# The order of VectorE's routing work in a linear attention with experts behind it, with POOL's tables in the third step and inputs loaded three items deep

## The chip, the cores and the metric

The kernel runs on one core of a Trainium2 chip. TensorE (PE, with its weight loads shown as PEld), VectorE (DVE), ScalarE (ACT), GpSimd (POOL) and SyncE (SP) each execute their own instructions in the order in which the program issues them, and wait for each other on semaphores; DMA transfers are issued from the queues of SP, ACT and POOL. The metric is device microseconds (us) of the whole program, the median of several runs. Before the change it is 382.65 us (3 runs, 382.16 to 382.88).

## The reference

A recurrent linear attention over 4 sequences, 8 heads, 768 tokens and a head dimension of 48, whose output is the input of a top-1 mixture of 8 experts (384 to 1024 to 384). A token keeps the expert of the token before it when its local gate is at least 0.5.

```python
for t in range(S):
    kt, vt, rt = (k[:, :, t], v[:, :, t], r[:, :, t])
    cur = np.einsum('bhd,bhe->bhde', u[None] * kt, vt)
    y[:, :, t] = np.einsum('bhd,bhde->bhe', rt, state + cur)
    state = w[None, :, :, None] * state + np.einsum('bhd,bhe->bhde', kt, vt)
...
for s in range(S):
    fresh_e = int(np.argmax(logits[b, s]))
    if s == 0 or local_gate[b, s] < 0.5:
        e = fresh_e
    else:
        e = prev_e if prev_e >= 0 else fresh_e
    prev_e = e
    ...
    h = np.maximum(x[b, s] @ w1[e], 0.0)
    out[b, s] = p[e] * (h @ w2[e])
```

## The kernel before

The attention works on 16 items, one for each sequence and pair of heads. An item is cut into 6 chunks of 128 tokens. Inside a chunk the scores (keys times queries, L288) are masked by `kept` (VectorE, `am`, L290) and multiplied with the values on PE (`inside`, L297); across chunks, PE sums keys and values of each chunk into T, a part of the PSUM bank `mp` (`added`, L248), a scan on VectorE turns T into the states S (`states`, L254), and PE multiplies them with the decayed queries `rw` (`before`, L310). The bonus term u is `own`: PE sums the product `pd` over the head dimension (L267) and VectorE multiplies it with the values vT (L273). POOL makes `rw`, `ke` and `pd` of the next item (`scale`, L212, L216, L229) and VectorE makes the scaled keys `kw` (`keys`, L236). Each result goes through ACT (L318) and is turned by PE (`turn`, L329), copied by ACT (L331) and stored to x_d. After the four items of a sequence, `logits` (L342, PE) and its copy lT (L343, ACT), then `token_logits` (L348 PE, L349 VectorE) give the gate logits `lt`.

The loop `run` (L352) goes over steps n = 0 to 16. Nothing is scheduled by the framework: the order of the source is the order on every engine. Step n does own(n), the scores of a later item, inside(n-1) and before(n-1), scale(n+1) on POOL and, from step 5, keys(n+2). Score tiles take turns on two pairs of PSUM banks (`banks`); turn, logits and token_logits use the same pairs, so each has to wait until the last reader of its pair is done.

Routing of the first two sequences (group 0; g = 8 in `run`) is woven into steps 9 to 15: `experts_of` (maximum L688, equality L689, its product with `down` L692, then L694 to L696), `keys` and `runs` (a transpose L703 and a scan L708), `turn_runs` (L713, into the last columns of `mp`), `last` (L720), `one_hot` (L727 to L731), `counts` (two matmuls into `mp`, L740 and L741), `ranks` (the ACT copy `ext` L747, the scan `exc` L748, `pos` and `far` L750 to L756), `slots` (L792 to L795), `columns` (`eqv`, L800), `numbers` (POOL, L805), `places` (`ohq`, L811, in two halves) and `summed` (L818). Its constants are made in `constants`, called in steps 3, 4 and 5: small integer tables by POOL's iota (L623), and memsets by VectorE; ACT casts the tables in step 6. The same functions are run again for group 1 in the experts' part, where POOL has no attention work.

Inputs come by SP: `load` (L189) issues rk (queries and keys of an item, 768 KB), kv (584 KB) and vT (384 KB) in this order. rk and vT have AHEAD buffers, kv has AHEAD + 1. Before the loop AHEAD - 1 items are loaded, then the small `wp`; step n loads item n + AHEAD - 1. A load into a buffer waits for that buffer's last reader: POOL's and VectorE's work on rk, the product in own on vT, inside on kv.

Behind step 16 the experts' part gathers tokens by indirect DMA and runs two small units and eight larger ones, bound by PE.

Of the kernel before, what the change touches and what calls it, by code (L numbers as in the profile page):

```python
# [14 lines left out]
Alu = mybir.AluOpType  # L15
# [5 lines left out]
P = 128  # L21
# [5 lines left out]
E, F = 8, 1024  # L27
DK, FK = D // P, F // P
NCH = S // P
NC = B * NCH  # L30
N = B * S

ST = 4
# [4 lines left out]
EARLY = 2  # L38
HEAD = 192
TAIL = 256  # L40
# [8 lines left out]

W_LO, W_HI = 0.8, 1.25  # L50
C2 = NCH // 2
AHEAD = 4
VB = NCH * 2 * DH


def spread(ap, axis, n):

    a = ap.unsqueeze(axis)
    return a.to_broadcast([n if i == axis else s for i, s in enumerate(a.shape)])


class Attention:
# [289 lines left out]
    def run(self, router, fetch, heads):  # L352


        def pair(name):
            t = self.banks(name)
            return [t[:, 0], t[:, 1]]

        M = B * HP

        mp, mp_end = router.mp, 2 * P + 2 + (NCH - 1) * DH

        g = GROUPS[0][1] * HP
        for n in range(M + 1):
            if n + AHEAD - 1 < M:
                self.load(n + AHEAD - 1)
            if n == 0:
                self.scale(0)
                self.keys(0)
                self.tables()  # L370
                self.scores(0, 0)()
                self.scores(0, 1)()
                self.own(0)
                self.nc.scalar.copy(self.first, self.tab[:, 1, 0])
                self.turn_ends(slice(1, HP))
                self.warm(3)
                self.added(0)
                self.reciprocals(1)
                self.states(0)
                self.scale(1)  # L380
                continue
            if n < 3:

                self.keys(n)
                self.inside(n - 1)
                self.before(n - 1)
                if n == 2:
                    self.turn(0, pair("tp"))
                self.nc.scalar.copy(self.first, self.tab[:, n + 1, 0])
                self.scores(n, 0)()  # L390
                keep = self.scores(n, 1)
                self.own(n)
                keep()
                self.added(n)
                self.states(n)
                if n == 1:
                    self.reciprocals(2)
                self.scale(n + 1)
                continue
            if n < M:  # L400
                self.turn(n - 2, pair("tp"))
                if n >= M - 2:
                    fetch(2 * (n - M + 2))
                if n == 3:
                    self.reciprocals(3)
                if n < 5:
                    self.keys(n)
                if n > 3:
                    if n not in (g + 3, g + 5):
                        self.added(n)  # L410
                    self.states(n)
            if n == 4:
                self.keys(5)
            if n > HP and n % HP == 1:
                self.token_logits(n // HP - 1, pair("lq")[0])
            if n == g + 1:
                router.experts_of(0, (0,))
            if n == g + 5:
                router.slots(0)
                router.columns(0)  # L420
            if n == M:
                router.shares(0)
            if n + 1 < M:
                self.scale(n + 1)
            if n == g + 6:
                router.numbers(0, self.nc.gpsimd)
            if 3 <= n < 6:
                router.constants(n - 3)
            if n == M:
                self.turn(M - 2, [self.spare[:, 0], self.spare[:, 1]])  # L430
            self.inside(n - 1)
            if n == g + 3:

                router.turn_runs(0, mp[:, mp_end:])
            self.before(n - 1)
            if M - 2 <= n < M:
                fetch(2 * (n - M + 2) + 1)
            if n == 6:
                router.cast()
            if n == M:  # L440
                break
            if n == g + 3:
                router.last(0, mp[:, mp_end:])
                router.one_hot(0, (0,))
            if n == g + 7:

                router.summed(0, 0)
                router.copied(0, self.nc.vector.tensor_copy)
                self.spare = self.py.tile([P, 2, 512], F32, name="y")
                router.head(self.spare[:, 0])  # L450
                heads()

            ahead = n if n < 5 else n + 1
            if n == 3:
                self.added(3)
                self.states(3)
            if ahead < M:
                self.scores(ahead, 0)()
                keep = self.scores(ahead, 1)
            if n % HP == 0:  # L460

                keep()
                self.own(n)
                self.logits(n // HP - 1, pair("lp")[0])
                if n == 4:
                    self.scores(5, 0)()
                    self.scores(5, 1)()
                    self.keys(6)
                if n == g + 4:
                    self.added(n + 1)  # L470
                    router.counts(0, [mp, mp[:, E * NC // 2:]])
                    router.ranks(0, (0,))
                if n > 4:
                    self.keys(n + 2)
                if n == g + 4:
                    router.ranks(0, (1,))
            else:
                self.own(n)
                if n == g + 2:
                    self.added(n + 1)  # L480
                    router.keys(0, mp)
                    router.runs(0)
                if 4 < n < M - 2:
                    self.keys(n + 2)
                if ahead < M:
                    keep()
            if n == g + 1:
                router.experts_of(0, (1,))
            if n == g + 3:
                router.one_hot(0, (1,))  # L490
            if n == g + 5:
                router.places(0, 0)
            if n == g + 6:
                router.places(0, 1)
        self.inner.close()
# [81 lines left out]
class Router:  # L577
# [43 lines left out]
    def iota(self, name, shape, pattern, base=0, cm=0, cast=False):  # L621
# [5 lines left out]
        self.casts.append((f, i))  # L627
        return f

    def constants(self, part):  # L630
        nc = self.nc
        if part == 0:
            self.ie = self.iota("ie", [P, E], [[1, E]])
            self.iq = self.iota("iq", [P, P], [[1, P]])
            self.ij = self.iota("ij", [P, E * ST], [[1, E * ST]])
            self.ones = self.tl("r_ones", [P, P])
            nc.vector.memset(self.ones, 1.0)
        elif part == 1:
            self.down = self.iota("down", [P, E], [[-1, E]], base=E, cast=True)

            self.t8 = self.iota("t8", [P, NC], [[E * P, NC]], base=2 * E, cm=E, cast=True)
            self.t1 = self.iota("t1", [P, NC], [[P, NC]], base=1, cm=1, cast=True)
        else:

            c = self.g[0]["nc"]
# [5 lines left out]
            nc.vector.memset(self.go, 1.0)  # L651
            nc.vector.memset(self.go.rearrange("p (b c) -> p b c", c=NCH)[:, :, NCH - 1:], 0.0)
            nc.vector.memset(self.g[0]["ext"][:, :, 0:1], 0.0)

            self.tie = self.tl("tie", [P, E])
            for x, (z, base) in enumerate(((slice(0, EARLY), E - 1 - E * TAIL), (slice(EARLY, E), E - 1 - EARLY))):
                i = self.iota(f"tie{x}", [P, z.stop - z.start], [[-1, z.stop - z.start]], base=base)
                self.casts.append((self.tie[:, z], i))
            self.ief = self.iota("ief", [1, E], [[1, E]], cast=True)

            self.size = self.tl("size", [1, E])
            for i, n in enumerate(BLOCKS):
# [18 lines left out]
    def experts_of(self, i, parts=(0, 1)):  # L681

        nc, g, lt = self.nc, self.g[i], self.lt
        lg = lt[:, g["z"], :E]
        if 0 in parts:
            nc.vector.memset(lt[:, g["z"]].rearrange("p (b c) e -> p b c e", c=NCH)[0:1, :, 0, E:], -1.0)
            mx = self.mp[:, :g["nc"]] if i == 0 else g["mx"]
            nc.vector.tensor_reduce(mx, lg, axis=AX.X, op=Alu.max)  # L688
            nc.vector.tensor_tensor(g["eq"], lg, spread(mx, 2, E), op=Alu.is_equal)  # L689
            if i == 0:  # L690
                nc.scalar.copy(g["mx"], mx)
            nc.vector.tensor_tensor(g["eq"], g["eq"], spread(self.down, 1, g["nc"]), op=Alu.mult)  # L692
        if 1 in parts:
            nc.vector.tensor_reduce(g["k"], g["eq"], axis=AX.X, op=Alu.max)  # L694
            nc.vector.tensor_tensor(g["k"], self.t8[:, g["z"]], g["k"], op=Alu.subtract)
            nc.vector.scalar_tensor_tensor(g["key"], lt[:, g["z"], E], FRESH_TO, g["k"],  # L696
                                           Alu.is_le, Alu.mult)
# [1048 lines left out]
```

## Time and profile before

| what | us |
|---|---|
| median of the runs | 382.65 |
| the profiled execution | 383.9 |
| span of the profiled execution | 382.2 |
| PE busy | 367.5 |
| DVE busy | 250.6 |
| POOL busy | 151.3 |
| ACT busy | 107.5 |
| the attention's part of the span, from its start to the experts' first transposes on PE (L1090) | 113.7 |

The span runs from the first to the last instruction of one profiled execution; the rest of its time lies around the span. A profile row "engine line waited for" names who waited and who ended the wait, with the total, the number and the longest. Spans on POOL are rough, and the ends of matmuls are modelled.

### The profile page before, as it was taken

How to read it: one execution, taken by the hardware profiler on the slowest of the kernel's cores; microseconds unless marked ns; L12 is line 12 of the kernel's file. 1: busy time of each engine (PE TensorE's matmuls, PEld its weight loads, DVE VectorE, ACT ScalarE, POOL GpSimd, SP SyncE). 2: the span in 40 equal slices, each digit the busy share in tenths (PEclk: the TensorE clock that was granted, in tenths of full speed). 3: DMA queues.
4: the chain of work that ended last, by engine and by line, in shares of the span. 5: the costliest groups of instructions: out<-in, count | busy, mean ns of one | idle time of the engine just before them, and what ended most of it. 6: DMA issues, size and time to landing. Idle time of an engine off the chain costs nothing. (4 is left out here: it accounts for less than half of the span.)

```text
span 382.2 us, 9693 instructions
## 1 busy us (share of the span) xinstructions
PE 367.5 (96%) x3846; PEld 324.1 (85%) x3846; DVE 250.6 (66%) x720; ACT 107.5 (28%) x295; POOL 151.3 (40%) x213
## 2 busy tenths in 40 slices
PE   7999999989999999999999999999999999999992
PEld 6776777766769998999999999999998899899971
DVE  6888778967945746496566857758758758466400
ACT  4132232223222212322422333233234233232210
POOL 8779999867222042311422313212323113012022
PEclk9999999989999999999999999999999999999997
DMA  7999999972566881720551254145246156064011
GB/s 262 409 410 410 408 396 327 358 272 91 189 223 209 317 352 41 306 107 22 211 204 62 63 190 192 51 173 207 76 166 228 37 178 228 10 215 170 3 37 36
DMA packets 17765, 74.97 MB, mean 196 GB/s; under 512 B 2761, under 2 KB 6618, under 8 KB 15408
## 3 DMA queue, kind: packets, MB, share of 16 engines
q1 hardware_dynamic: 10336, 56.89, 39.9%
q0 software_dynamic: 3424, 9.52, 7.5%
q10 hardware_dynamic: 3952, 7.87, 5.7%
q8 instruction: 32, 0.52, 0.5%
q14 instruction: 21, 0.17, 0.1%
HBM read 64.83 MB, written 9.51 MB: 195 GB/s over the span
## 5 line engine op out<-in xcount | busy, mean ns | idle before, releaser
L1303 POOL DMA_INDIRECT out_dram<-yo,sid x27 | 26.6, 987 | 102.4 <-ACT yo L1298 79.0
L1154 PE MATMUL h<-exT,w1t 128*128 128x168 f32 (+4 forms) x240 | 54.9, 327 | 0.0
L1158 DVE TENSOR_TENSOR hT<-h,hs 128x168 f32<-128x168 f32 (+3 forms) x60 | 21.1, 351 | 46.5 <-PE h L1154 31.0
L1077 POOL DMA_INDIRECT xg<-x_d,gid x29 | 31.1, 1073 | 37.1 <-DVE sm L900 17.4
L1154 PEld LDWEIGHTS h<-exT,w1t 128*128 128x128 f32 x240 | 41.6, 190 | 0.3 <-issue 0.3
L1104 PE MATMUL h<-exT,w1t 128*128 128x192 f32 (+1 forms) x192 | 38.3, 338 | 0.0
L1223 PE MATMUL y<-factors,sums 128*128 128x192 f32 x168 | 36.8, 326 | 0.0
L216 POOL TENSOR_TENSOR pd<-rk 128x384 f32<-128x384 f32 x32 | 31.3, 999 | 10.2 <-PE y L267 7.6
L1154 PE MATMUL h<-xs,ws 128*128 128x168 f32 (+4 forms) x144 | 35.2, 326 | 0.0
L290 DVE TENSOR_TENSOR am<-pair,kept 128x768 f32<-128x768 f32 x32 | 30.0, 951 | 6.7 <-PE pair L288 6.1
L1104 PEld LDWEIGHTS h<-exT,w1t 128*128 128x128 f32 x192 | 32.3, 190 | 1.5 <-issue 0.2
L1154 PEld LDWEIGHTS h<-xs,ws 128*128 128x128 f32 x144 | 25.5, 190 | 4.3 <-ACT hs L1161 1.2
L1223 PEld LDWEIGHTS y<-factors,sums 128*128 128x128 f32 x168 | 28.9, 190 | 0.0
L212 POOL TENSOR_TENSOR ke<-kv,endT 128x288 f32<-128x288 f32 x32 | 25.0, 800 | 0.7 <-DMA kv<-in_kv_dram 0.7
L297 PE MATMUL y<-am,kv 128*64 128x128 f32 x360 | 23.9, 276 | 0.8 <-DVE y L273 0.8
L288 PE MATMUL pair<-rw,kw 48*64 48x128 f32 (+1 forms) x768 | 23.2, 253 | 1.4 <-DVE lt L349 0.6
L229 POOL TENSOR_TENSOR rw<-rk,tab 128x384 f32<-128x384 f32 x26 | 23.5, 924 | 2.1 <-DMA rk<-in_rk_dram 2.1
L1223 PE MATMUL y<-w2t,hT 128*128 128x192 f32 x96 | 23.0, 328 | 0.0
L288 PEld LDWEIGHTS pair<-rw,kw 48*64 48x64 f32 x768 | 19.7, 135 | 3.6 <-issue 1.2
L1091 DVE COPY exT<-tp 128x384 f32<-128x384 f32 (+6 forms) x29 | 14.0, 488 | 12.9 <-PE tp L1090 12.7
L297 PEld LDWEIGHTS y<-am,kv 128*64 128x64 f32 x360 | 20.0, 137 | 2.4 <-DVE y L273 1.0
L318 ACT COPY xT<-y 128x768 f32<-128x768 f32 x15 | 12.0, 801 | 34.0 <-PE y L310 34.0
(300 smaller groups left out, 740.4 us busy)
## 6 DMA issues: line engine op xcount, KB each, us to landing
w1t<-in_w_dram SPq DMA_DIRECT2D x8, 1536.0 KB, 6.6
w2t<-in_w_dram SPq DMA_DIRECT2D x8, 1536.0 KB, 7.1
rk<-in_rk_dram SPq DMA_DIRECT2D x15, 768.0 KB, 9.9
kv<-in_kv_dram SPq DMA_DIRECT2D x16, 584.0 KB, 8.4
vT<-in_vT_dram SPq DMA_DIRECT2D x16, 384.0 KB, 7.8
x_d<-x ACTq DMA_DIRECT2D x4, 1152.0 KB, 8.2
w1t<-in_w_dram SPq DMA_DIRECT2D x2, 768.0 KB, 4.6
w2t<-in_w_dram SPq DMA_DIRECT2D x2, 768.0 KB, 5.3
```

The costliest lines, as they stand in the source:

```text
L212: nc.gpsimd.tensor_mul(t["ke"][:, p::2], t["k"][:, p::2], spread(self.endT[:, p, hp], 1, C2))
L216: nc.gpsimd.tensor_mul(t["pd"][:, z], t["rT"][:, z], t["kT"][:, z])
L229: engine.tensor_mul(t["rw"][:, z], t["rT"][:, z], spread(pw, 1, z.stop - z.start))
L288: nc.tensor.matmul(sc[f * DP:(f + 1) * DP, h, i, x:], lhsT=t["kw"][q, c, o * DP:(o + 1) * DP], rhs=t["rw"][q, c, x:], start=True, stop=True)
L290: return lambda: nc.vector.tensor_mul(t["am"][:, g], sc, spread(self.kept[:, g:g + 3], 1, 2))
L297: nc.tensor.matmul(t["y"][h][p * DP:(p + 1) * DP, c2 * P:(c2 + 1) * P], lhsT=t["v"][:, (2 * c + h) * DH:(2 * c + h) * DH + DP], rhs=t["am" ...
L1077: self.nc.gpsimd.indirect_dma_start(out=xg[:n], out_offset=None, in_=self.x_d[:rows], in_offset=bass.IndirectOffsetOnAxis(ap=u["gid"][:n, ...
L1104: nc.tensor.matmul(h[:, :n], lhsT=u["w1"][:, m, kk, :], rhs=u["xT"][:, kk, :], start=(kk == 0), stop=(kk == DK - 1))
L1154: nc.tensor.matmul(out, lhsT=a, rhs=b, start=start and k == 0, stop=stop and k == len(terms) - 1, skip_group_check=True)
L1158: nc.vector.tensor_tensor(out, a, b, op=Alu.add)
L1223: return lambda: nc.tensor.matmul(bank[:, x * half:(x + 1) * half], lhsT=a, rhs=b, start=(j == 0 and x == 0), stop=(j == FK // 2 - 1), ski ...
L1303: self.nc.gpsimd.indirect_dma_start(out=out.rearrange("n (h d) -> (n h) d", h=2) if half else out, out_offset=bass.IndirectOffsetOnAxis(ap ...
```

## The change

The number of input buffers goes from 4 to 3 (kv from 5 to 4), which also puts the load of `wp` in front of item 2's. POOL's iotas move from steps 3, 4 and 5 into one new function, `numbering`, called in step 2 between states(2) and scale(3); the memsets of `constants` stay in steps 3 and 5. In step 9 the equality of group 0 is written to PSUM (free columns of `mp`) in place of SBUF, and the product with `down` reads it there. The scan states(11) moves from the start of step 11 to step 10, behind runs and in front of keys(12). In step 12 added(13) and counts stand in front of logits on PE instead of behind it. `columns` moves from step 13's slots to the end of step 13, and `places(0, 0)` from there into step 14, behind numbers.

```diff
@@ -49,7 +49,7 @@
 
 W_LO, W_HI = 0.8, 1.25
 C2 = NCH // 2
-AHEAD = 4
+AHEAD = 3
 VB = NCH * 2 * DH
 
 
@@ -395,6 +395,8 @@
                 self.states(n)
                 if n == 1:
                     self.reciprocals(2)
+                else:
+                    router.numbering()
                 self.scale(n + 1)
                 continue
             if n < M:
@@ -408,7 +410,8 @@
                 if n > 3:
                     if n not in (g + 3, g + 5):
                         self.added(n)
-                    self.states(n)
+                    if n != g + 3:
+                        self.states(n)
             if n == 4:
                 self.keys(5)
             if n > HP and n % HP == 1:
@@ -417,14 +420,14 @@
                 router.experts_of(0, (0,))
             if n == g + 5:
                 router.slots(0)
-                router.columns(0)
             if n == M:
                 router.shares(0)
             if n + 1 < M:
                 self.scale(n + 1)
             if n == g + 6:
                 router.numbers(0, self.nc.gpsimd)
-            if 3 <= n < 6:
+                router.places(0, 0)
+            if n in (3, 5):
                 router.constants(n - 3)
             if n == M:
                 self.turn(M - 2, [self.spare[:, 0], self.spare[:, 1]])
@@ -461,14 +464,15 @@
 
                 keep()
                 self.own(n)
+                if n == g + 4:
+                    self.added(n + 1)
+                    router.counts(0, [mp, mp[:, E * NC // 2:]])
                 self.logits(n // HP - 1, pair("lp")[0])
                 if n == 4:
                     self.scores(5, 0)()
                     self.scores(5, 1)()
                     self.keys(6)
                 if n == g + 4:
-                    self.added(n + 1)
-                    router.counts(0, [mp, mp[:, E * NC // 2:]])
                     router.ranks(0, (0,))
                 if n > 4:
                     self.keys(n + 2)
@@ -480,6 +484,7 @@
                     self.added(n + 1)
                     router.keys(0, mp)
                     router.runs(0)
+                    self.states(n + 1)
                 if 4 < n < M - 2:
                     self.keys(n + 2)
                 if ahead < M:
@@ -489,7 +494,7 @@
             if n == g + 3:
                 router.one_hot(0, (1,))
             if n == g + 5:
-                router.places(0, 0)
+                router.columns(0)
             if n == g + 6:
                 router.places(0, 1)
         self.inner.close()
@@ -627,19 +632,24 @@
         self.casts.append((f, i))
         return f
 
+    def numbering(self):
+        self.ie = self.iota("ie", [P, E], [[1, E]])
+        self.iq = self.iota("iq", [P, P], [[1, P]])
+        self.ij = self.iota("ij", [P, E * ST], [[1, E * ST]])
+        self.down = self.iota("down", [P, E], [[-1, E]], base=E, cast=True)
+        self.t8 = self.iota("t8", [P, NC], [[E * P, NC]], base=2 * E, cm=E, cast=True)
+        self.t1 = self.iota("t1", [P, NC], [[P, NC]], base=1, cm=1, cast=True)
+        self.tie = self.tl("tie", [P, E])
+        for x, (z, base) in enumerate(((slice(0, EARLY), E - 1 - E * TAIL), (slice(EARLY, E), E - 1 - EARLY))):
+            i = self.iota(f"tie{x}", [P, z.stop - z.start], [[-1, z.stop - z.start]], base=base)
+            self.casts.append((self.tie[:, z], i))
+        self.ief = self.iota("ief", [1, E], [[1, E]], cast=True)
+
     def constants(self, part):
         nc = self.nc
         if part == 0:
-            self.ie = self.iota("ie", [P, E], [[1, E]])
-            self.iq = self.iota("iq", [P, P], [[1, P]])
-            self.ij = self.iota("ij", [P, E * ST], [[1, E * ST]])
             self.ones = self.tl("r_ones", [P, P])
             nc.vector.memset(self.ones, 1.0)
-        elif part == 1:
-            self.down = self.iota("down", [P, E], [[-1, E]], base=E, cast=True)
-
-            self.t8 = self.iota("t8", [P, NC], [[E * P, NC]], base=2 * E, cm=E, cast=True)
-            self.t1 = self.iota("t1", [P, NC], [[P, NC]], base=1, cm=1, cast=True)
         else:
 
             c = self.g[0]["nc"]
@@ -651,12 +661,6 @@
             nc.vector.memset(self.go, 1.0)
             nc.vector.memset(self.go.rearrange("p (b c) -> p b c", c=NCH)[:, :, NCH - 1:], 0.0)
             nc.vector.memset(self.g[0]["ext"][:, :, 0:1], 0.0)
-
-            self.tie = self.tl("tie", [P, E])
-            for x, (z, base) in enumerate(((slice(0, EARLY), E - 1 - E * TAIL), (slice(EARLY, E), E - 1 - EARLY))):
-                i = self.iota(f"tie{x}", [P, z.stop - z.start], [[-1, z.stop - z.start]], base=base)
-                self.casts.append((self.tie[:, z], i))
-            self.ief = self.iota("ief", [1, E], [[1, E]], cast=True)
 
             self.size = self.tl("size", [1, E])
             for i, n in enumerate(BLOCKS):
@@ -686,10 +690,11 @@
             nc.vector.memset(lt[:, g["z"]].rearrange("p (b c) e -> p b c e", c=NCH)[0:1, :, 0, E:], -1.0)
             mx = self.mp[:, :g["nc"]] if i == 0 else g["mx"]
             nc.vector.tensor_reduce(mx, lg, axis=AX.X, op=Alu.max)
-            nc.vector.tensor_tensor(g["eq"], lg, spread(mx, 2, E), op=Alu.is_equal)
+            eq = self.mp[:, g["nc"]:g["nc"] * (E + 1)].rearrange("p (c e) -> p c e", e=E) if i == 0 else g["eq"]
+            nc.vector.tensor_tensor(eq, lg, spread(mx, 2, E), op=Alu.is_equal)
             if i == 0:
                 nc.scalar.copy(g["mx"], mx)
-            nc.vector.tensor_tensor(g["eq"], g["eq"], spread(self.down, 1, g["nc"]), op=Alu.mult)
+            nc.vector.tensor_tensor(g["eq"], eq, spread(self.down, 1, g["nc"]), op=Alu.mult)
         if 1 in parts:
             nc.vector.tensor_reduce(g["k"], g["eq"], axis=AX.X, op=Alu.max)
             nc.vector.tensor_tensor(g["k"], self.t8[:, g["z"]], g["k"], op=Alu.subtract)
```

## The prediction

> **What bounds the kernel now.** I read the page first, then the busy time by stretches, then PE's waits in the attention, then the order of time around each wait.
>
> ```profile
> span 382.2 us, 9693 instructions
> PE 367.5 (96%) x3846; PEld 324.1 (85%) x3846; DVE 250.6 (66%) x720; ACT 107.5 (28%) x295; POOL 151.3 (40%) x213
> PEclk9999999989999999999999999999999999999997
> ```
>
> PE is busy for 96% of the span, so only PE's remaining waits and its granted clock can be won. The one clock digit of 8 before the end lies near 80 us. The diff touches the attention alone, 0 to 113 us; behind it PE shows no wait on another engine, so I let the experts' part move as a block.
>
> ```profile
> 18.00:50.00 32.00, 31.20 (x687) 23.54 (x688) 25.78 (x56) 8.32 (x21) 29.25 (x43) 1.00 1.02 409
> 50.00:68.00 18.00, 17.88 (x401) 13.38 (x397) 14.93 (x20) 5.51 (x15) 18.00 (x22) 1.00 0.95 351
> 68.00:84.00 16.00, 14.35 (x272) 10.65 (x270) 13.01 (x22) 3.38 (x8) 11.91 (x15) 0.89 0.92 338
> 84.00:113.00 29.00, 27.13 (x561) 20.64 (x564) 21.81 (x39) 8.21 (x21) 14.64 (x17) 1.00 0.54 175
> ```
>
> The columns are the stretch, its length, busy time of PE, PEld, DVE, ACT and POOL, PEclk, DMA share and GB/s. From 18 to 68 us PE misses 0.9 us of 50, although POOL and DMA look full. From 68 to 113 it misses 3.5 us of 45 and loses clock. That is where this change can act, and this says on what PE waited there:
>
> ```profile
> PE pair L329 <- DVE am L290: 1.4, 2, 0.7
> PE mp L713 <- DVE inc L726: 1.0, 1, 1.0
> PE pair L288 <- DVE lt L349: 0.6, 1, 0.6
> PE y L828 <- DVE rows L824: 0.5, 1, 0.5
> ```
>
> VectorE ends all of them. Below I go by the steps n of the attention loop; own(n) (L267) starts at 60.65 for n = 8, then 67.94, 73.89, 81.33, 87.77, 96.06, 102.12 and 108.11.
>
> **Loads three deep: 0.** The next item's rk now waits until POOL and DVE have read the item three before it, and vT until own of that item. Through item 8 the old landings are a queue of 4.3 us per item (rk at 30.28, 34.53, 38.82, 43.15); the new issue times (about 21.5, 27.4, 33.0, 38.5) are before each transfer's turn, and POOL wants them at 33.36, 38.73, 44.35 and 49.43. The wp load goes ahead of item 2: 128 of 1736 KB, 0.3 us on POOL's pd(2), which own(2) wants 2 us later. Later, loads come one item late: kv(12) lands near 74.2 where POOL reached it at 72.83, rk(13) near 77.7 instead of 76.87. That costs POOL about 1.4 us, hidden by the 3.0 us it then waits for own(11) before pd at 83.02. Bounds 0 and, if that cover is gone, 1.4 us; I take 0.
>
> **Tables in the third step: 0.** Nine iotas of 0.12 to 0.22 us (0.96 us of POOL's time: 0.41, 0.29 and 0.26 where they stood) go in front of scale(3).
>
> ```profile
> POOL rw L229 <- DMA rk<-in_rk_dram: 2.1, 1, 2.1
> POOL ke L212 <- DMA kv<-in_kv_dram: 0.7, 1, 0.7
> ```
>
> There POOL idles 2.1 us for rk(3), which covers them. POOL ends 0.96 us sooner in steps 4 to 6, but PE never waits for POOL there, rw being ready 2 to 3 us early, so nothing is won. Without the cover, pd(3) ends at most 0.96 us later; it ended at 26.92 and own(3) started at 28.61, so still 0. The DVE memsets stay in their steps.
>
> **eq in PSUM, step 9: 0.6 won.**
>
> ```profile
> 65.57 0.25 DVE L689 TENSOR_TENSOR eq<-lt,mp 128x96 f32<-128x96 f32 x1
> 65.86 2.67 DVE L692 TENSOR_TENSOR eq<-eq,down 128x96 f32<-128x96 f32 x1
> 68.46 0.94 DVE L290 TENSOR_TENSOR am<-pair,kept 128x768 f32<-128x768 f32 x1
> L692 DVE TENSOR_TENSOR eq<-eq,down x2: 257/1465/2673, 65.9 to 116.1; 128x96 f32<-128x96 f32 x2
> ```
>
> The same line takes 0.257 us at 116 us, where POOL is still, and 2.673 us here, ending 0.1 us behind POOL's last multiplication of a run (rw, rw, ke, ke, to 68.42). L689, with one input in PSUM, takes 0.25 us beside the same POOL work. With eq in PSUM L692 has that form: 2.4 us less of DVE. What is late next is PE: the am behind it needs scores(10,0), ready at 67.54, so am comes 0.9 us earlier, and PE's wait at L329 (0.65 us, 68.81 to 69.46) goes. In step 10 DVE is tight (kw, am, L694 to L696, S), and L695 and L696 still read SBUF twice (0.73 and 0.72 us against 0.17); bounds 0 and 0.65, I take 0.6. The Trainium skill ("SBUF — State Buffer", Who interferes with whom) says that a VectorE instruction with two SBUF inputs and a GpSimd instruction that reads SBUF exclude each other, the later one waiting until the first finishes. By that rule L692 had only to wait for the rw half ending at 66.09, some 0.5 us in all, and this term would be 0; the row shows it passed over at three boundaries, so the row decides.
>
> **S(11) one step earlier: 1.0 won, and with it the clock: 1.4.**
>
> ```profile
> 78.60 0.23 PE L713 MATMUL mp<-ident,run 12*128 12x12 f32 x1 [1.00 <-DVE inc L726]
> 79.91 1.68 PE L288 MATMUL pair<-rw,kw 48*64 48x128 f32 x48
> 81.33 1.54 PE L267 MATMUL y<-pd,w_t 48*64 48x384 f32 x8
> 77.10:80.50 3.40, 2.40 (x59) 1.96 (x59) 1.81 (x6) 0.96 (x2) 2.96 (x4) 1.00 0.96 304
> 80.50:83.90 3.40, 3.40 (x46) 2.14 (x38) 2.07 (x4) 0.22 (x2) 0.88 (x1) 0.51 0.75 308
> ```
>
> L713 writes mp and starts as the scan S(11), which reads mp, ends at 78.55; run itself was ready at 76.27. Moved up behind runs, S(11) ends before 77, and PE goes on at 77.60: 1.0 us. Queued behind the moved scan are kw(12) and am(11,1), each 0.65 us later, am until 78.64; scores(12,0) wants that bank near 78.9, 0.3 us of room. Bounds 0.7 and 1.0.
> Directly behind this wait the granted clock is 0.51 for 3.4 us. I price it by the rows under full clock beside it: scores 1.68 against 1.45, own 1.54 against 0.88, turn 1.34 against 0.79, 1.44 us in all. In the stretch before the drop PE streamed little: tiny L713 and L720, and the gap. Filled with 1 us of scores it resembles 94.20 to 97.60, where PE waited 1.3 us and kept its clock. I take 1.4; bounds 0 (it drops all the same) and 1.7 (half of 3.4).
> The Trainium skill ("TensorE: Matmul & The Clock Gate", HAM oscillation) gives as its rule that PE gaps beyond some 3.4 us make the clock fall. By it a gap of 1.0 us would be harmless, the drop would have another cause and stay, and the sum would be 1.4 us higher; but the trace's only drop in the attention stands right behind its longest gap.
> Against this, L728 (two SBUF inputs) now meets POOL's rw(13), where POOL idled before: up to one half of rw, 0.85 us, of which PE feels about 0.25 at turn(10). Bounds 0 and 0.85.
>
> **Counts before logits, columns later: 0.1 lost.** PE does the same work in another order. ACT, however, keeps lT (0.48 us) ahead of ext, and lT now waits for the later logits: exc asks 0.57 us later. It already waited for POOL (1.08 us here, 0.37 at 126 us) until a boundary at 92.44; I estimate 0.4 later, felt at the scores that wait for lt (L288, 0.63). Then eqv (0.56) no longer stands before am(14,0): 0.5 back, less what is rounded in the overlaps. Bounds 0.5 won and, if exc is passed over until POOL rests at 94.02 as L692 was, 1.6 lost.
>
> **places(0,0) in step 14: 0.7 lost.** am(15,0) started at 101.72, just when its scores were ready, 1.49 us behind the end of am(14,1). Between them now stand columns 0.5, S 0.65 and ohq 0.9, plus up to 0.3 if ohq meets POOL's numbers, which start when columns ends: 2.05 to 2.35. PE's turn(13) needs that am to end; own(14) leaves 0.2 us of room. Bounds 0.4 and 0.75; I take 0.7, as the two will meet.
>
> **Sum.** 0.6 + 1.0 + 1.4 − 0.25 − 0.1 − 0.7 = 1.95, taken as 1.9 us. The profiled execution took 383.9 us, 382.2 of span and 1.7 around it, so it would become 382.0; it lies 1.25 above the median of the runs, 382.65, which becomes 380.8.
>
> **Rivals.** (1) The clock drops anyway, there or a window later, because PE's activity and not the one gap decides; for it, the work around 77 to 80 us stays thin; against it, similar stretches at 66.9 and 94.2 kept the clock. Then 0.5 us is left: 382.1, within what counts as no change. (2) The end on the other side: VectorE's two-input operations are passed over by POOL at new places. The place is exc in step 12: POOL runs pd, rw, ke without a pause from 88.83 to 94.02, and if exc gets in only there the lt reduction and with it PE's scores are 1.6 us late; a PE wait of over 2 us in one window then costs a clock drop, 1.4. 382.65 − 1.9 + 1.6 + 1.4 = 383.75. It decides from a delay of about 1.2 us with a drop. Against it: at 72.85, 73.60, 85.95 and 92.44 such operations got in at the next boundary. (3) Three-deep loads starve POOL where I see 1.4 us of delay under 3.0 of cover; if an x_d write doubles the delay, 2 us reach PE and the result is 382.7 or more, up to 384. (4) The changed order does nothing, DVE in step 10 taking back all that step 9 gave: 0.6 less, 381.4, which the range holds.
>
> **How the numbers follow.** Forecast with (4) 0.55, (1) 0.22, (2) 0.17, (3) 0.06. A measurement of this kernel can tell about 0.2%, 0.77 us, from no change. Faster: 0.55 and a little of (1), 0.57. Same: most of (1) and some of (3), 0.20. Slower: (2) and the rest, 0.23. The forecast's own range is 379.5 (best ends: 0.65, 1.0, 1.7, no cost in steps 11 and 12, 0.4 in 14: 2.95, and noise) to 381.8. The range with the rivals reaches to 383.7.
>
> **What would show it.** After the change: L692 at 0.26 us; no PE wait at L713 and no clock digit of 8 near 80 us; own(12) 2 to 2.7 us earlier than 87.77; POOL waiting for DMA at kv(12) and rk(13) yet no PE wait on POOL; PE's wait at the scores behind lt (L288) 0.6 to 1.1 us; a new PE wait at L329 near 101 us of 0.4 to 0.75 us. A clock drop elsewhere, or exc over 1.5 us, would make the prediction wrong.

## The result, with the profile after

The changed kernel takes 383.55 us in the median (14 runs, 381.76 to 389.19); the kernel before took 383.04 us beside it on the same chip (14 runs, 382.16 to 384.90). The ratio is 1.001 with a 95% interval of 0.9988 to 1.0031: no change that can be measured, where a gain of 1.9 us was forecast. Medians and ranges are those of all runs, but each ratio and each spread below leaves out the runs that are over 1.5% longer than the shortest of their kernel (389.19 here, two each in e2, e4 and e6 and one in e5, with e4's profiled execution among them). What did change is the spread, 5.5 us in place of 2.7. The profiled execution took 385.6 us, 2.0 above its median, so it shows a larger loss than the median run has. Its page:

```profile
span 383.8 us, 9693 instructions
PE 369.4 (96%) x3846; PEld 324.8 (85%) x3846; DVE 251.3 (65%) x720; ACT 107.2 (28%) x295; POOL 151.7 (40%) x213
PEclk9999999999899999999999999999999999999997
```

The clock digit of 8 has moved from the slice near 80 us to the one near 97. The busy time by stretches, with the columns of the prediction (stretch, length, busy time of PE, PEld, DVE, ACT and POOL, PEclk, DMA share, GB/s):

```profile
18.00:50.00 32.00, 31.36 (x693) 23.81 (x697) 26.29 (x56) 8.43 (x22) 31.45 (x45) 1.00 0.98 373
50.00:68.00 18.00, 18.00 (x405) 13.47 (x397) 13.82 (x21) 5.41 (x14) 17.42 (x21) 1.00 0.93 310
68.00:84.00 16.00, 15.52 (x330) 12.10 (x326) 14.43 (x24) 4.08 (x10) 12.68 (x15) 1.00 0.96 378
84.00:113.00 29.00, 26.00 (x503) 19.01 (x495) 21.52 (x36) 7.15 (x19) 13.57 (x15) 0.94 0.65 221
```

From 68 to 84 us PE now misses 0.5 us where it missed 1.65, at full clock. From 84 to 113 it misses 3.0 us where it missed 1.9, and the clock went there. The starts of own(n) say the same by steps:

| n | 8 | 9 | 10 | 11 | 12 | 13 | 14 | 15 | experts' first h |
|---|---|---|---|---|---|---|---|---|---|
| before | 60.65 | 67.94 | 73.89 | 81.33 | 87.77 | 96.06 | 102.12 | 108.11 | 115.22 |
| after | 60.27 | 67.55 | 72.83 | 79.65 | 85.34 | 96.05 | 102.86 | 108.84 | 116.08 |

Up to own(12) the forecast gain was there, 2.43 us, of which 0.38 had come before own(8). Between own(12) and own(13) it was lost: 10.71 us against 8.29. Half a microsecond more went at own(0), 9.49 against 9.00, where the change does nothing. Another 0.8 us went behind the experts' first h, which the prediction had let move as a block: from there to the end of the span it is 267.75 us against 266.97, with one new wait of PE for ACT (L1196, below). That is not the change either: the profiled executions of e5 to e11, with three and with four items, all have 267.8 to 267.9 there, and e1 to e4 and e12 have 267.0. What PE waited for after the change:

```profile
PE pair L288 <- DVE far L759: 1.8, 1, 1.8
...
PE pair L329 <- DVE am L290: 0.7, 2, 0.3
PE pair L288 <- DVE lt L349: 0.7, 1, 0.7
PE y L1196 <- ACT hT L1112: 0.5, 1, 0.5
PE y L833 <- DVE rows L829: 0.5, 1, 0.5
```

The wait at L713 (now L718) is gone, and the wait of 1.8 us at L288 is new. DVE and POOL in time order around it (start, duration, instruction, idle time before and its releaser), first DVE:

```profile
89.56 3.17 DVE L753 TENSOR_TENSOR_SCAN exc<-seg,ext 128x104 f32<-128x104 f32 x1 [1.93 <-ACT ext L752]
```

and POOL in the same stretch:

```profile
89.26 1.73 POOL L229 TENSOR_TENSOR rw<-rk,tab 128x384 f32<-128x384 f32 x2
90.90 1.60 POOL L212 TENSOR_TENSOR ke<-kv,endT 128x288 f32<-128x288 f32 x2
```

The scan exc takes 0.37 us where POOL is still, at 127 us. Here it took 3.17, and got its turn only when the fourth of POOL's multiplications beside it had ended, at 92.50, behind which POOL rested. Everything behind it on VectorE, kw and far and the reduction lt, came 2.8 us late, PE waited 1.8 and 0.7 us for it, and then the clock fell, as the two stretches show:

```profile
92.85:96.25 3.40, 1.48 (x52) 1.31 (x56) 3.26 (x12) 0.28 (x1) 0.00 (x0) 1.00 0.49 174
96.25:99.66 3.41, 3.41 (x38) 1.97 (x31) 2.75 (x4) 0.77 (x3) 1.97 (x2) 0.50 0.03 7
```

So in this execution the prediction's second rival happened at the place that it named, and both of the signs that were to prove the prediction wrong, a clock drop elsewhere and exc over 1.5 us, were there. The experiments ask why there, why not in every run, and which part of the change brought it.

### The profile page after: what moved, and what is told of

It reads as the page before. It is cut to its first block, busy times and chain, and to the rows that moved or that the text cites. A ratio compares the mean times of both kernels' runs of the same rounds, so it can differ in the third digit from the quotient of the medians.

```text
span 383.8 us, 9693 instructions
## 1 busy us (share of the span) xinstructions
PE 369.4 (96%) x3846; PEld 324.8 (85%) x3846; DVE 251.3 (65%) x720; ACT 107.2 (28%) x295; POOL 151.7 (40%) x213
## 5 line engine op out<-in xcount | busy, mean ns | idle before, releaser
L288 PE MATMUL pair<-rw,kw 48*64 48x128 f32 (+1 forms) x768 | 23.0, 249 | 2.8 <-DVE far L759 1.8
L288 PEld LDWEIGHTS pair<-rw,kw 48*64 48x64 f32 x768 | 19.2, 133 | 5.4 <-issue 4.0
```

The lines of the kernel that those rows point to most:

```text
L288: nc.tensor.matmul(sc[f * DP:(f + 1) * DP, h, i, x:], lhsT=t["kw"][q, c, o * DP:(o + 1) * DP], rhs=t["rw"][q, c, x:], start=True, stop=True)
```

## The experiments

Each kernel was timed beside the kernel before on its own chip; ratios are to that. "3" and "4" are the values of AHEAD.

| run | loads | median us (range, runs) | ratio, 95% interval |
|---|---|---|---|
| the change | 3 | 383.55 (381.76 to 389.19, 14) | 1.001, 0.9988 to 1.0031 |
| e1_exc_psum | 3 | 385.19 (384.52 to 386.2, 8) | 1.0068, 1.0039 to 1.0097 |
| e2_logits_first | 3 | 383.91 (381.16 to 390.49, 12) | 1.0019, 0.9981 to 1.0057 |
| e3_ahead4 | 4 | 381.43 (380.81 to 381.78, 12) | 0.9973, 0.9956 to 0.999 |
| e4_places_back | 3 | 384.67 (381.67 to 388.18, 12) | 1.0032, 0.9996 to 1.0068 |
| e5_three_deep_only | 3 | 384.34 (382.99 to 388.81, 12) | 1.0025, 0.9992 to 1.0059 |
| e6_psum_inputs_3 | 3 | 382.17 (380.6 to 387.05, 12) | 0.9982, 0.9947 to 1.0017 |
| e7_psum_inputs_4 | 4 | 381.66 (381.25 to 383.23, 12) | 0.9963, 0.9939 to 0.9986 |
| e8_scan_and_eq | 4 | 382.23 (381.67 to 384.22, 12) | 0.997, 0.9941 to 0.9998 |
| e9_rk_three_deep | rk 3, vT 4 | 384.46 (382.44 to 384.73, 6) | 1.0029, 1.0002 to 1.0056 |
| e10_pool_filler_4 | 4 | 389.18 (388.87 to 390.04, 5) | 1.0165, 1.0138 to 1.0192 |
| e11_best | 4 | 382.23 (381.36 to 382.94, 6) | 0.9979, 0.9953 to 1.0004 |
| e12_places_back_4 | 4 | 382.16 (381.27 to 385.82, 12) | 0.9999, 0.9974 to 1.0024 |

**e1: exc without its second SBUF input.** The counts are written to PSUM in the layout that exc reads, so that exc has one input in PSUM and the copy ext falls away. The memset of the gaps was put behind one_hot's second part.

```diff
+ gap = mp[:, E * NC // 2:E * NC // 2 + E * (NC // 2 + 1)].rearrange("p (e c) -> p e c", e=E)
+ self.nc.vector.memset(gap[:, :, 0:1], 0.0)
...
- g["ext"].rearrange("p e c -> p (e c)"), 0.0, Alu.mult, Alu.add)
+ g["ext"].rearrange("p e c -> p (e c)") if i else g["tt"], 0.0, Alu.mult, Alu.add)
```

> The changed kernel with one difference: group 0's counts are written by PE straight into the layout that the scan exc reads, so exc has one input in PSUM and ACT's copy ext falls away. Theory (exc with two SBUF inputs is kept out by POOL until POOL rests, and PE's wait behind it drops the clock): exc takes 0.37 to 0.45 us in place of 3.17, the PE wait of 1.8 us at the scores of step 13 goes, own(13) starts near 92.5 in place of 96.05, no clock drop in the attention, and the time is 380.0 to 381.5, 1.5 to 3 us under the kernel before, with little spread. Rival (the order of counts and logits, or the loads three deep, costs the time): exc gets short but own(13) stays after 94 and the time within 0.8 us of before.

exc took 0.36 us beside POOL's pd, as wanted. The time was lost elsewhere, by this edit itself. VectorE's part of the trace:

```profile
82.84 1.08 DVE L738 TENSOR_TENSOR oh<-ei,ie_i 128x96 f32<-128x96 int32 x1
83.93 0.07 DVE L497 MEMSET mp<- 128x8 f32 x1
```

and PE's:

```profile
84.09 1.04 PE L248 MATMUL mp<-kv,ke 128*48 128x48 f32 x20 [2.92 <-POOL rw L229]
```

The memset stands on VectorE behind kw, am and oh, and added(12) writes the bank of the memset. Of PE's 2.9 us POOL's hold of oh is 0.8 (1.08 against 0.25 in e4); the rest is the memset's place. added(12) started 0.09 us after the memset had ended; the releaser that the row names, POOL, had ended a multiplication at 83.81 and the next only at 84.80. The clock was at half from 83.72 to 87.13. This says that exc can be freed, and nothing of what that is worth.

**e2: step 12's order alone undone.**

```diff
- if n == g + 4:
-     self.added(n + 1)
-     router.counts(0, [mp, mp[:, E * NC // 2:]])
  self.logits(n // HP - 1, pair("lp")[0])
  ...
  if n == g + 4:
+     self.added(n + 1)
+     router.counts(0, [mp, mp[:, E * NC // 2:]])
      router.ranks(0, (0,))
```

> The changed kernel with step 12's order undone (logits, then added and counts). Theory (POOL keeps exc out): exc asks some 0.5 us earlier, still inside POOL's run of pd, rw and ke, so it still takes 2 to 3.5 us whenever it is passed over; time 382 to 384. Rival (the new order is what costs, because ext stands behind lT on ACT): exc starts 0.6 us earlier and is short, time 380.5 to 381.5.

The median is that of the change within the intervals, and the spread is as wide (5.1 us). The profiled execution was one of the short ones (381.3): exc, asked at 89.00, took 0.52 us. The order in step 12 is not what makes the spread.

**e3: four items ahead again, the rest of the change kept.**

```diff
-AHEAD = 3
+AHEAD = 4
```

> The changed kernel with loads four deep again. Theory: POOL no longer waits for kv(12) and rk(13), ends its run of rw and ke 0.5 to 1.5 us earlier in step 12, so exc is kept out a little shorter; time within 1 us of the changed kernel, 382 to 384. Rival (three-deep loads starve POOL and so PE): 380.5 to 381.5 and exc short.

The rival of that expectation held: 0.9973, and 12 runs within 1.0 us. DVE at the two operations that were in doubt:

```profile
79.07 0.85 DVE L733 TENSOR_TENSOR ei<-inc,rn 128x12 int32<-128x12 f32 x1
...
89.70 0.67 DVE L753 TENSOR_TENSOR_SCAN exc<-seg,ext 128x104 f32<-128x104 f32 x1 [1.93 <-ACT ext L752]
```

and POOL beside the first of them:

```profile
78.34 1.56 POOL L212 TENSOR_TENSOR ke<-kv,endT 128x288 f32<-128x288 f32 x2
80.73 1.97 POOL L216 TENSOR_TENSOR pd<-rk 128x384 f32<-128x384 f32 x2 [0.83 <-PE y L267]
```

With the inputs there in time POOL reaches ke's end at 79.90 and rests 0.83 us for own(11). L733 gets in there at the latest. In e8, e9 and e12, which have four buffers for vT, it got in at such a rest too (0.8 to 1.3 us long). In the changed kernel POOL was at rw in that place, behind a wait of 0.32 us for DMA, and ran on; L733 got in all the same, in 0.34 us, and in e1 and e2 in 0.78 and 0.88. In e4, next, it didn't.

**e4: columns and the first places back where they were, still three deep.**

```diff
  router.slots(0)
+ router.columns(0)
...
- router.places(0, 0)
...
- router.columns(0)
+ router.places(0, 0)
```

> The changed kernel with columns and places(0,0) where they stood before. Theory: PE's turn near 103 us no longer waits for am(15,0), but the scores of step 14 wait 0.5 us longer behind eqv; net -0.3 to +0.3 us, so 382 to 384 and exc as long as in the changed kernel. Rival (their order is what costs): 381 to 382.

The median did not move from the change's by more than the intervals. Its profiled execution (388.18) is the longest of its twelve runs, and shows at its plainest what can happen. DVE:

```profile
77.86 6.64 DVE L733 TENSOR_TENSOR ei<-inc,rn 128x12 int32<-128x12 f32 x1
```

POOL:

```profile
77.47 1.70 POOL L229 TENSOR_TENSOR rw<-rk,tab 128x384 f32<-128x384 f32 x2
79.11 1.55 POOL L212 TENSOR_TENSOR ke<-kv,endT 128x288 f32<-128x288 f32 x2
80.61 1.95 POOL L216 TENSOR_TENSOR pd<-rk 128x384 f32<-128x384 f32 x2
82.51 1.95 POOL L229 TENSOR_TENSOR rw<-rk,tab 128x384 f32<-128x384 f32 x2
```

An operation on 12 numbers per partition, 0.17 us alone (L728 in the kernel before), took 6.64 us, through eight multiplications with no pause between them, and ended 0.03 us behind the last. PE waited 6.0 us for the am behind it (L329), and the clock was at half for 6.8 us. This is the operation that the prediction bounded at 0.85.

**e5: three deep alone, in the kernel before.** The edit of e3 the other way round, in the old kernel.

> The kernel before with loads three deep and nothing else. Theory (late loads push POOL's rw, ke and pd of items 12 to 14 together into one run without a pause, and VectorE's operations with two SBUF inputs are kept out of it): L728, which took 0.17 us in the kernel before, takes 0.8 us or more in some executions, and the time is 383.5 to 386 with a spread of several us; PE shows no wait on a load and none on POOL. Rival (three-deep loads cost only together with the new order): 382 to 383 and as little spread as before.

The median rose by 0.25% (about 1.0 us), not clear of nothing by its interval. The profiled execution (383.9, which is 0.4 under the median) does not show the theory: L728 took 0.17 us, as before, and between 60 and 104 us no operation of VectorE with two SBUF inputs took more than 1.22. What this execution lost stands earlier. own(8) came at 61.50 us against 60.65 before, because PE stopped for 1.2 us between two matmuls of `added` near 46 us:

```profile
PE mp L248 <- issue: 1.2, 1, 1.2
q8 instruction: 32, 0.52, 0.5%
```

No semaphore ends this wait. The second line, from the page, names what it goes with: instructions come by DMA, here in 32 packets of 16 KB (0.52 MB). That these are PE's own is not stated there; it is read from what follows. In the 14 profiled executions take the two steps from own(5) to own(7), and for each the packet that lands nearest to its start. The step lasts 5.28 to 5.30 us in the 11 cases where the packet has landed by 0.16 us behind own(n), 5.52 to 5.60 in the 12 with 0.33 to 0.61, 5.84 to 5.87 in the 4 with 0.62 to 0.92, and 6.61 in this one, with 1.63. No run varied this, so it is a very close agreement and not an experiment; why the packet came late here is not shown.

So e5 has the higher median, but does not show that VectorE made it. As to the spread, the kernels with three items ahead (the change, e2, e4, e5, e6) cover 4.9 to 5.5 us in 10 to 13 runs, e1 apart, whose eight runs all lie high. Those with four cover 1.0 to 2.6 us, e12 4.6 by a single run, and the kernel before 4.4 in the 35 runs beside e5 to e8. The width of the middle half of the runs tells more than these ends: it is 1.4 to 3.8 us with three items, 0.4 to 1.3 with four, and 0.7 in those 35 runs.

**e6 and e7: the disputed inputs in PSUM, three and four deep.** exc as in e1, with the memset moved to step 10 behind the scan S(11), and inc written to PSUM so that L733 (here L737) too has one input there; e7 is e6 with AHEAD = 4.

```diff
+ if i == 0:
+     g["inc"] = self.mp[:, 216:216 + g["nc"] + 1]
```

> The changed kernel, loads three deep, where two of VectorE's operations get an input in PSUM: inc (read by L733) and exc's counts (without ACT's copy ext). Theory (keeping out is the cost of three-deep loads, and these two are the places that decide): L733 takes 0.17 and exc 0.37 us, the time is 380.5 to 382 and the spread under 2 us. Rival (late loads cost by themselves, or other operations are kept out instead): 383 or more, or a spread as wide as the changed kernel's.

> The same two inputs in PSUM with loads four deep. Theory: 0.3 to 1.0 us under e3_ahead4's 381.43, as L733 (0.86 there) and exc (0.67, and its wait for ext) get short: 380.4 to 381.1. Rival (nothing is left to win there, PE being bound otherwise): 381.2 to 381.6.

Three deep, DVE of e6 shows both freed while POOL was multiplying:

```profile
78.35 0.17 DVE L737 TENSOR_TENSOR ei<-mp,rn 128x12 int32<-128x12 f32 x1
...
86.65 0.36 DVE L760 TENSOR_TENSOR_SCAN exc<-seg,mp 128x104 f32<-128x104 f32 x1
```

The ratio fell from the change's 1.001 to 0.9982, within the intervals, but the spread stayed at 5.0 us, where the theory had under 2. Other operations that work from SBUF alone are left in the same steps, as key, oh, L738 (0.54 us here against 0.17) and pos; that these keep it wide is not shown, and the rival, that late loads cost by themselves, is not excluded by this run. Four deep the spread went, and the ratio of 0.9963 can't be told from e3's.

**e8: what eq and the moved scan are worth alone**, in the kernel before, four deep.

```diff
+ if n != g + 3:
      self.states(n)
...
+ self.states(n + 1)
...
- nc.vector.tensor_tensor(g["eq"], lg, spread(mx, 2, E), op=Alu.is_equal)
+ eq = self.mp[:, g["nc"]:g["nc"] * (E + 1)].rearrange("p (c e) -> p c e", e=E) if i == 0 else g["eq"]
+ nc.vector.tensor_tensor(eq, lg, spread(mx, 2, E), op=Alu.is_equal)
```

> The kernel before with only the scan S(11) moved and eq in PSUM. The prediction's terms for these two and the clock (0.6, 1.0 and 1.4, less 0.25) give 2.7 us under the kernel before, 379.5 to 380.5, with own(12) 2.5 us earlier and no clock drop near 80 us. Rival (step 12's and 14's reorders, which this leaves out, are neutral, and the two parts are worth what e3_ahead4 won): 381.2 to 381.7. If the clock drops somewhere else: 381.5 to 382.5.

0.3%, or 1.15 us (0.1 to 2.3 by the interval), where the prediction's terms for these parts came to 2.75 us with the clock. own(8) to own(12) took 24.40 us; in the profiled execution of before it took 27.12, and in e5's, which has the old step 9 and the old scan but no clock drop, 25.36. By steps, in the order before, e5, e8: 9 to 10 takes 5.95, 5.28 and 5.28, as L692 was held for 2.67 us in the first and for 1.22 in the second; 10 to 11 takes 7.44, 7.24 and 6.40; 11 to 12 takes 6.44, 5.56 and 5.45. So eq gave 0.67 us against the long hold and nothing against the short one, the scan about 0.8, and the clock drop had cost about 1.1 (0.20 and 0.88). The profiled execution of e8 is the longest of its twelve runs (384.22), with a clock drop of its own at 96 us; three of the twelve have its mean clock of 0.991. The drop near 80 us was in the one execution of before that had been profiled, and the mean clock suggests that few others have one: of the 35 runs of before beside e5 to e8, 6 have a mean granted clock of 0.992 or less, the others 0.993 or more.

**e9: three deep for rk alone**, with four buffers for vT and five for kv.

```diff
-rk, vT, kv = self.rks[n % AHEAD], self.vTs[n % AHEAD], self.kvs[n % (AHEAD + 1)]
+rk, vT, kv = self.rks[n % AHEAD], self.vTs[n % VT], self.kvs[n % KV]
```

> The changed kernel with only rk three deep; vT has four buffers and kv five, as in the kernel before. Theory (the loads come late because rk stands behind a vT in SP's queue, which waits for own of the item three before; rk's own buffer is free in time): rk(13) is issued near 66 in place of 71.2 us, POOL does not wait for it, and the time is that of loads four deep, 381.0 to 382.0 (0.996 to 0.999 of before), with few long executions. Rival (rk's depth itself is what counts): as the changed kernel, 383 to 384.

rk(13) landed at 74.2, POOL no longer waited for it, L734 (L733 in e3) took 0.86 us and exc 0.67, as in e3. In time this was no gain, since PE lost 2.1 us in steps 4 to 8, which run at 9.93, 5.84, 5.84 and 6.12 us against 9.44, 5.59, 5.28 and 5.28 in e3. PE's wait there:

```profile
PE mp L249 <- issue: 2.0, 4, 0.7
```

No semaphore that the profile shows ends it. It goes with the packets of instructions as in e5: they landed 0.77, 0.90 and 1.07 us behind own(5), own(6) and own(7). Why they came later than in e3 is open.

**e10: late loads without late loads.** e3 with two more multiplications of 128x384 on POOL behind rw of item 12, into a buffer that nobody reads.

```diff
+ if n == 12 and what is rw:
+     for i in range(2):
+         nc.gpsimd.tensor_mul(self.junk, t["rT"][:, :C2], t["kT"][:, :C2])
```

> Loads four deep, the new order, and two multiplications more on POOL (128x384, about 1 us each, their result unused) behind rw of item 12, which makes POOL's ke and pd of item 12 and all of item 13 late by the 1.5 to 2 us that the late loads cost. No load is late. Theory (POOL's pause is what counts, not the loads as such): L733 meets POOL's run of rw, ke, pd and is kept out for over 0.9 us in some executions; the time rises from 381.4 to 382.5 to 384.5 with a spread of several us. Rival (late transfers cost in another way): no change from 381.4 and little spread.

1.7 us more of POOL's work (153.3 us busy against 151.6), on an engine that is busy for 40% of the span, cost 7.3 us (the ratio 1.0165 less e3's 0.9973), and all five runs lie within 1.2 us. DVE, POOL and PE, one view each:

```profile
83.22 7.12 DVE L740 TENSOR_TENSOR oh<-ei,ie_i 128x96 f32<-128x96 int32 x1
90.27 0.64 DVE L258 TENSOR_TENSOR_SCAN S<-step,mp 128x240 f32<-128x240 f32 x1
```

```profile
83.22 1.96 POOL L233 TENSOR_TENSOR rw<-rk,tab 128x384 f32<-128x384 f32 x2
85.15 1.53 POOL L213 TENSOR_TENSOR ke<-kv,endT 128x288 f32<-128x288 f32 x2
86.65 1.93 POOL L217 TENSOR_TENSOR pd<-rk 128x384 f32<-128x384 f32 x2
88.55 1.67 POOL L233 TENSOR_TENSOR rw<-rk,tab 128x384 f32<-128x384 f32 x2
```

```profile
91.01 1.04 PE L252 MATMUL mp<-kv,ke 128*48 128x48 f32 x20 [4.94 <-POOL rw L233]
```

oh, 0.25 us in e4, got in when POOL rested, at 90.2. The theory held in kind, but not in place, since it named L733, which took 0.54 us, nor in size, since it had 382.5 to 384.5 and a wide spread. Behind oh stood the scan S, and behind that PE, which writes the bank that S reads. The row names POOL's rw as the releaser, but PE started 0.10 us behind S: the releaser was VectorE. No load was late in this part of the kernel: POOL ran from 68.81 to 90.22 us without a pause, where in e3 it rested at 80 and at 86 us, and that was enough.

**e11: e7 with the first places moved behind own(14) in the source.**

> e7_psum_inputs_4 with places(0,0) between own(14) and the last am of step 14 in place of in front of am(15,0). Theory (the term of 0.4 to 0.75 for places(0,0) in step 14 is real: e7 shows own(14) to own(15) at 6.64 us against 5.98 in the kernel before): PE's wait of 0.7 us at L329 near 99 us goes, own(14) to own(15) takes 6.0 us and the time is 380.8 to 381.3. Rival (the wait moves to the matmuls of summed): 381.4 to 381.9.

The wait at L329 in step 14 went, and PE waited 0.9 us for S at summed instead; 14 to 15 took 6.85 us. Not better than e7.

**e12: e4's edit four deep.**

> The changed kernel with four items of input in flight again and with the columns and the first places in the steps where they stood before (columns behind slots, places at the end of the next step). Everything else of the change stays. Theory (places in step 14 cost PE 0.7 us at the scores behind am(15,0)): step 14 to 15 is back near 6.0 us in place of 6.5, and the time is 0.4 to 0.7 us under that of four items with all of the change, so a ratio near 0.995 to 0.996 against 0.9973 there. In step 11 the row of 12 elements (L733) meets rw at one boundary at most, below 1 us. Rival (what step 14 pays is saved in step 13, where columns and places stood in front of am(14,0)): 13 to 14 is longer by as much, own(15) comes at the same time, ratio 0.997 to 0.998. Second rival (four items leave no pause where places stand before): a two-input row of over 2 us and a ratio over 1.

Step 14 to 15 is back at 5.98 us from 6.52 in e3, and 13 to 14 is 6.07 where e3 has 5.41: what the change pays in step 14 it saves in step 13. L733 took 0.95 us. The ratio of 0.9999 is above e3's with overlapping intervals. Part of it may be a wait that this profiled execution alone shows,

```profile
112.74 0.88 PE L1095 MATMUL tp<-ident,xg 128*128 128x128 f32 x6 [1.66 <-DMA xg<-x_d,gid]
```

where the first gather took 6.3 us from issue to landing against 4.6 in e3. Whether the timed runs had it too can't be seen.

## Why the prediction was wrong, step by step

**The step that failed: "Loads three deep: 0."** Its rows were right. POOL waits for DMA where it said, for rk in 1.4 us and for kv in 0.5 between 68 and 90 us, and behind the start of the span no wait of PE on POOL stands in the list of waits. What it took from them was wrong: it asked whether late data would reach PE through POOL and set POOL's 3.0 us of idle time against it as cover. That idle time had a second use, as it let VectorE's operations on SBUF in. The profiled execution of the change (exc held for 3.17 us), e4 (6.64 us), e3 (spread and loss gone with four items) and e10 (a loss of the same kind with no load late) show it. The term put at 0 measured 1.4 us by the change against e3 (1.001 less 0.9973) and 1.0 by e5's median, each known to about 1 us; e5's profiled execution lost its time at PE's instructions and not on VectorE, so how much of the term in the median is VectorE's is not shown. Single runs of the change reach 387.28. The bound of 1.4 us fell with it, and so did the 0.85 for the operation that is now L733: "up to one half of rw" became eight halves in e4.

**Rival (2) at 0.17 and rival (3) at 0.06 were one mechanism.** (2) had exc's place, and its 1.6 us was 1.9 in the profiled execution (1.8 and 0.7, less the 0.6 that PE waited there before), with the clock drop behind it; but it was given to the new order of step 12; e2 shows that this order isn't needed. (3) had the right part of the change, but looked for it in waits of PE on POOL. Had the two been put together, the question would have been how many two-input operations meet an unbroken run of POOL, and the chance would have been larger. That (2)'s 383.75 lies near the median of 383.55 is chance: the execution that shows (2) took 385.6.

**The clock term, "1.4", was mis-sized: about 1.1 in the profiled execution, and near 0 in the median.** The drop near 80 us was real, and it did go. By e8, which won 1.15 us with all three parts, little or nothing of it was in the median. The prediction had the clue and only noted it: the profiled execution lay 1.25 us above the median, nearly this term.

**eq in PSUM and S(11) earlier, 0.6 and 1.0 less 0.25, were right in kind**: L697 took 0.26 us and the wait at L713 is gone. Between own(8) and own(12) they gave 0.96 us against e5's execution and about 1.6 against that of before, with its longer hold; in the time it was 1.15 with all that the clock did, against 1.35.

**Counts before logits, 0.1, and places(0,0), 0.7: together near 0 in place of 0.8 lost.** PE's wait behind lt was 0.4 us in e3. ohq met POOL's numbers (1.31 us against 0.95) and step 14 lost 0.54, as the term said. The saving in front of am(14,0), taken as 0.5 and mostly set off against exc, was 0.66 in e12's comparison.

**Tables in the third step, 0**: own(0) to own(4) takes 25.79 us in the change and 25.78 before, so the cover held. Step 6 to 7 takes 5.28 us in the change and in e1 to e4, e6 and e12, and 5.56 to 5.59 in the three kernels with the old places (before, e5, e8). That is not shown to be a gain of the tables: e7, e9 and e11 have the new places and take 5.58 to 5.84, and the step follows the landing of PE's instructions, as in e5's part.

By the medians the sum is then 1.15 won by eq and the scan, 0 for the orders, and 1.0 to 1.4 lost by three items: between 0.15 won and 0.25 lost, where 0.4 lost was measured. With terms known to about 1 us each, this is agreement and no proof.

**What stays open.** Which phase between VectorE and POOL lets an operation in at the next boundary: in e3 exc met the same unbroken run of rw and ke and took 0.67 us, in the change 3.17. That the timing of the DMA makes POOL's phase vary from run to run with three items, and that this is the spread, is argued from the spreads and from POOL's waits, not shown run by run. Late packets of instructions are a second cause that the spread may have, and no run separates the two. Why these packets came late in e5 and e9 is open. What the memory saved by three items is for was not tried.

**The versions that measured faster than the kernel before** are the change with four items, e3, at 0.9973 (0.9956 to 0.999), e7 at 0.9963 (0.9939 to 0.9986), and e8 at 0.997 (0.9941 to 0.9998).

## What to carry to other kernels

Idle time of a helper engine can be what lets another engine work: before it is spent as cover, look for operations of VectorE on SBUF alone that stand beside it, and for how long POOL runs on without a pause. A term that rests on one profiled execution is worth no more than its share of the runs, so set that execution against the median before pricing what is peculiar to it. Where PE stops and no semaphore ends the wait, its instructions may have landed late. And where the spread grows while the median stays, an average over runs hides a mechanism that a single profile may or may not show.

## What the runs showed of the hardware

A VectorE operation with both inputs in SBUF was either let in at one of the next two ends of a POOL multiplication or not before POOL stopped. In the profiled executions of this case there are four of the second kind: 2.67 us (eq, before), 3.17 (exc, after), 6.64 (L733, e4) and 7.12 (oh, e10), each ending 0.03 to 0.23 us behind the last of four to eight multiplications in a row. The Trainium skill ("SBUF — State Buffer", Who interferes with whom) has the later of two such instructions wait until the first finishes; these four rows waited for up to eight, so here the rule is a lower bound. An operation with one SBUF input and no second one was held too: L734 took 0.79 us beside POOL in the change and 0.17 in e3.

The granted clock fell to half for 3.4 us, or 6.8, right behind stretches of 3.4 us in which PE was busy for 1.48 us (the change), 1.99 (e8) and 2.40 (before), though not behind the one from 94.20 to 97.60 in before, with 2.14, so PE's busy time alone does not decide it. The pair of e8:

```profile
92.50:95.90 3.40, 1.99 (x46) 1.22 (x39) 3.23 (x9) 0.62 (x1) 0.94 (x1) 1.00 0.64 227
95.90:99.40 3.50, 3.50 (x45) 3.22 (x45) 3.50 (x5) 0.77 (x3) 1.81 (x3) 0.51 0.30 69
```

PE had two waits of 0.7 us there, and in the change one of 1.8 and one of 0.7. The Trainium skill ("TensorE: Matmul & The Clock Gate", HAM oscillation) ties such drops to gaps beyond some 3.4 us; only e4's 6.0 and e10's 4.9 us were that long.
